# An mLSTM cell with a feed-forward block: the cells of chunks 2 to 5 beside groups 1 and 2, and groups 3 to 5 in three float32r parts

## The chip, the cores and the metric

The kernel runs on one core of one Trainium2 chip. The metric is the device time of one execution in microseconds. Before the change the median of three runs is 528.26 us (527.74 to 528.6).

A core has a matrix engine (TensorE, PE in the profile; the loading of its stationary operand is PEld), three engines for elementwise work (VectorE, DVE; ScalarE, ACT; GpSimd, POOL) and SyncE (SP), whose queue starts nearly all DMA transfers of this kernel. Each engine works through its own instructions in order and waits for the others by semaphores. SBUF is the on-chip memory, PSUM the memory into which TensorE writes, DRAM the memory outside.

## What is computed

The first half is a recurrent cell with a matrix state, 4 batches x 8 heads, 768 tokens, head dimension 40:

```
for t in range(S):
    m_new = maximum(f_gate[t] + m, i_gate[t])
    f_stab = exp(f_gate[t] + m - m_new);  i_stab = exp(i_gate[t] - m_new);  m = m_new
    C = f_stab * C + i_stab * outer(v[t], k[t])
    n = f_stab * n + i_stab * k[t]
    y[t] = sigmoid(o_gate[t]) * (C @ q[t]) / maximum(abs(n . q[t]), 1)
```

Its output, (B, H, S, D), becomes x of 3072 tokens x 320, and a feed-forward block follows: `h = x @ w_in` (320 x 2048), `g = max(0.01 h, h)`, `out = g @ w_out` (2048 x 320). Inputs are float32, the two weight matrices float64, which the kernel reads as 64-bit words and narrows to float32 itself.

## The kernel before

Tokens are cut into 6 chunks of 128. A *visit* s is one chunk c of one batch b (s = 4 c + b, 24 visits). The state of a batch passes from visit s to visit s + 4, so chunks follow each other. A *group* g of the feed-forward block is the 4 x 128 tokens of chunk g. In the main loop (L945) group c - 1 is computed beside the cells of chunk c, and the last group alone.

A group is a list of 32 units (`ff_units`). The first 16 are the entry: for each of 8 j, two units that together multiply x by two blocks of 128 columns of w_in (L743). x lies in `xT` in two halves of 64 rows, so the two blocks (r = 0 and 1) run as two matmuls of 64 rows and 512 columns side by side; ACT applies the leaky ReLU and writes `acts` (L751). The last 16 units are the exit: 16 matmuls of 320 columns for each 128 tokens (L778), a copy by ACT (L786) and a store (L787).

A visit of chunks 2 to 5 has two places where it uses TensorE:

- `u_parts` (scores L598, state update L603) needs the transposed keys and queries `kqT` (VectorE, L489), the decay weights `w` and `ku`, and gives `sd`; VectorE multiplies by `w` (L608) and adds to the state (L580).
- `u_mix` (L679) needs that, and gives `pT`. VectorE transposes it to `hb` (L686), forms the denominators (L617 to L619), multiplies by the output gate (L690), POOL by the denominators (L693), VectorE transposes to `x` (L697), and SP stores it in DRAM as `x_dr` (L700). `gather_x` reads it back into `xT` (L714).

After a u_mix of visit s comes `ahead(s + 2)`: kqT and `qn` of visit s + 2 (L489, L495), its `ku` and decayed state on POOL (L462, L576), and SP's loads of k, q and `ea` for visit s + 4. Then `load_late` and `feed` start o of visit s + 2 and k, v and `w` of visit s + 4. v goes in four transfers straight into the state tile S (L343). `prep_mask` adds the causal mask to w on POOL (L434), `prep_exp` takes the exponentials on ACT (L442).

`pairs` says after which unit of the group the cell units are done: two u_parts after unit 2, two u_mix after 6, two u_parts after 14, two u_mix after 19.

PE, DVE, ACT and POOL run in the order in which the code writes the instructions; SP's order is put together by the framework from when each transfer can start. `cells`, `wk`, `consts` and `gates` are pools of SBUF memory; all live for the whole kernel.

Of the kernel before, what the change touches and what calls it, by code (L numbers as in the profile page):

```python
# [9 lines left out]
F32 = mybir.dt.float32  # L10
U32 = mybir.dt.uint32
# [3 lines left out]
PSUM = bass.MemoryType.PSUM  # L15


@with_exitstack
def kernel(
# [51 lines left out]
    assert KR == DP and KC == 5 and KC * DP == Dm and GT * 4 <= 2048  # L71

    consts = ctx.enter_context(tc.tile_pool(name="consts", bufs=1))
    gp = ctx.enter_context(tc.tile_pool(name="gates", bufs=1))
    wk = ctx.enter_context(tc.tile_pool(name="wk", bufs=2))
    psf = ctx.enter_context(tc.tile_pool(name="psf", bufs=4, space=PSUM))
    psc = ctx.enter_context(tc.tile_pool(name="psc", bufs=4, space=PSUM))
# [47 lines left out]
    acts = consts.tile([P, NF, GT], F32, name="acts")  # L125
# [36 lines left out]
    QN = NF // 4  # L162
    QC = 4 * P
    WC = KC * 2 * P
    w_in = consts.tile([P, QN, WC], F32, name="w_in")
    w_out = consts.tile([P, NF, Dm], F32, name="w_out")
# [5 lines left out]
    def w_row(r, slot, j):  # L172
        n, e = divmod(j, 2)
        at = (2 * slot + e) * P
        return w_in[DP * r : DP * (r + 1), n, at : at + P]
# [6 lines left out]
    HW = 2 * Dm  # L182
    wide = moe_w_in.dtype == U64
    raws = {}
    if wide:
        raw_t = consts.tile([P, 5 * HW], U64, name="raw")

    def load_weights(n):

        m = n - QN  # L190
        if n < QN:
            dst = w_in[:, n, :]
        else:
            dst = w_out[:, 2 * m : 2 * m + 2, :].rearrange("p a d -> p (a d)")
        to = dst
        if wide:
            if n < 2:
                at = NF * GT - 2 * WC * (n + 1)
                raw = acts_l[:, at : at + 2 * WC].bitcast(U64)
            elif n < QN:  # L200
                raw = raw_t[:, WC * (n - 2) : WC * (n - 1)]
            elif m < 2:
                raw = w_out[:].rearrange("p f d -> p (f d)")[:, (2 + m) * WC : (3 + m) * WC].bitcast(U64)
            else:
                at = (4, 0, 1, 2, 3, 4)[m - 2] * HW
                raw = raw_t[:, at : at + HW]
            raws[n] = (raw, dst)
            to = raw
# [11 lines left out]
    def narrow_weights(n):  # L220
# [3 lines left out]
        if not wide:  # L224
            return
# [102 lines left out]
    def load(s):  # L328
# [12 lines left out]
        for u in range(2):  # L341
            for i in range(2):
                nc.sync.dma_start(  # L343
# [687 lines left out]
```

## Time and profile before

| | us |
|---|---|
| median of three runs | 528.26 |
| span of the profiled execution, first to last instruction | 526.4 |
| start to the first unit of group 1 | 139.64 |
| chunks 2, 3, 4, each with a group | 78.8 |
| chunk 5 with group 4 | 78.0 |
| group 5 alone, to the last instruction of TensorE | 69.3 |
| TensorE busy | 513.2 |
| VectorE, ACT, POOL busy in chunk 4 (78.76) | 32.7, 20.3, 17.4 |

The profile is one execution. "Busy" is the time in which an engine executes; an idle engine costs nothing unless the engine that sets the end waits for it. A matmul's weight load is a record of its own (PEld) and overlaps the matmuls before it. In a timeline a row is start, duration, engine, line and operation, and in brackets how long the engine stood idle before it and what ended that.

### The profile page before, as it was taken

To read this page: it belongs to the slowest core of one execution; us is meant where nothing else is said; L and a number is where in the kernel's file an instruction comes from. 1 tells how busy PE (TensorE), PEld (TensorE's weight loads), DVE (VectorE), ACT (ScalarE), POOL (GpSimd) and SP (SyncE) were. 2 spreads that over 40 slices of the span, in tenths; PEclk is the share of its full clock that TensorE was granted. 3 is DMA by queue.
4 is the path that set the end of the run, shared out by engine and by line. 5 is a ranking of instruction groups with operands and counts; after the bars stand their busy time and mean duration, and the time that the engine had idled before them with its cause. 6 is when DMAs were issued, how large, how long until landed. Compare 5 with 4: busy or idle time off the path is not lost.

```text
span 526.4 us, 11333 instructions
## 1 busy us (share of the span) xinstructions
PE 513.2 (97%) x4501; PEld 336.3 (64%) x4501; DVE 240.3 (46%) x431; ACT 168.1 (32%) x458; POOL 113.0 (21%) x145
## 2 busy tenths in 40 slices
PE   8889989999999999999999999999999999999997
PEld 7877878777555577555577555577554577544675
DVE  4679998999328446028445028344028230000000
ACT  4565865534534212034212124212125100122100
POOL 4244354152205121015021015021013010000000
PEclk9668999999999999999999999999999999999999
DMA  9977687888755626685626676626542112000000
GB/s 116 156 204 153 138 212 171 196 145 175 146 137 105 137 72 150 129 174 107 138 75 143 134 150 129 138 76 155 125 102 52 50 52 87 14 0 1 12 12 25
DMA packets 165284, 59.13 MB, mean 112 GB/s; under 512 B 128816, under 2 KB 156016, under 8 KB 165232
## 3 DMA queue, kind: packets, MB, share of 16 engines
q1 hardware_dynamic: 164848, 58.28, 51.0%
q8 instruction: 35, 0.57, 0.5%
q10 hardware_dynamic: 384, 0.13, 0.1%
q14 instruction: 17, 0.14, 0.1%
HBM read 51.68 MB, written 6.70 MB: 111 GB/s over the span
## 4 chain that ended last, share of the span: by engine, by line
PE 83%; SPq 6%; DVE 4%; DMA 2%; ACT 2%; issue 1%; POOL 1%; ACTq 0%; POOLq 0%
PE po L778 38%; PE ph L743 36%; PE pT L679 3%; SPq L213 3%; PE sd L598 3%; SPq L338 2%; SPq L352 1%; PE sd L603 1%; DMA rb<-in_q_dram 1%; DVE raw L245 1%; DVE qn L608 1%; DMA S<-in_v_dram 0%; DMA raw<-in_moe_w_in_dram 0%; PE tk L518 0%; PE hN L649 0%
## 5 line engine op out<-in xcount | busy, mean ns | idle before, releaser
L743 PE MATMUL ph<-xT,w_in 64*128 64x512 f32 (+1 forms) x1120 | 215.2, 536 | 0.6 <-ACT acts L751 0.6
L778 PE MATMUL po<-w_out,acts 128*128 128x320 f32 x768 | 211.1, 434 | 0.0
L778 PEld LDWEIGHTS po<-w_out,acts 128*128 128x128 f32 x768 | 144.5, 190 | 62.6 <-issue 4.1
L743 PEld LDWEIGHTS ph<-xT,w_in 64*128 64x128 f32 x1120 | 107.8, 189 | 94.4 <-issue 87.7
L751 ACT ACTIVATE acts<-ph 128x512 f32<-128x512 f32 (+1 forms) x112 | 53.9, 534 | 151.8 <-PE ph L743 151.7
L608 DVE TENSOR_TENSOR qn<-w,sd 64x512 f32<-64x512 f32 x40 | 27.4, 684 | 97.7 <-PE sd L603 57.1
L576 POOL TENSOR_TENSOR S<-S,f 40x336 f32<-40x336 f32 x36 | 30.9, 858 | 101.9 <-PE pT L679 65.8
L442 ACT ACTIVATE w<-w,gT 128x64 f32<-128x64 f32 (+1 forms) x192 | 51.1, 348 | 3.1 <-POOL w L434 2.1
L434 POOL TENSOR_TENSOR w<-w,i 128x512 f32<-128x512 f32 x20 | 28.1, 1411 | 104.7 <-ACT bu L294 53.0
L786 ACT COPY y<-po 128x320 f32<-128x320 f32 x12 | 5.1, 423 | 83.3 <-PE po L778 83.3
L786 ACT COPY hn<-po 128x320 f32<-128x320 f32 x12 | 5.1, 426 | 76.0 <-PE po L778 76.0
L686 DVE STREAM_TRANSPOSE hb<-pT 128x512 f32<-128x512 f32 x16 | 11.4, 714 | 39.2 <-PE pT L679 39.0
L495 DVE TENSOR_TENSOR qn<-kqT,ea 64x512 f32<-64x512 f32 x32 | 27.3, 854 | 0.9
L693 POOL TENSOR_TENSOR xb<-xb,den 128x320 f32<-128x320 f32 x16 | 11.7, 728 | 66.5 <-DVE xb L690 66.5
L598 PEld LDWEIGHTS sd<-kqT 40*64 40x64 f32 x640 | 19.9, 135 | 6.1 <-issue 6.1
L697 DVE STREAM_TRANSPOSE x<-xb 128x512 f32<-128x512 f32 x16 | 18.1, 1130 | 7.7 <-POOL xb L693 7.7
L598 PE MATMUL sd<-kqT 40*64 40x64 f32 x640 | 21.5, 220 | 0.0
L603 PE MATMUL sd<-S,vu 64*40 64x42 f32 x576 | 20.1, 214 | 0.7 <-POOL vu L462 0.7
L489 DVE STREAM_TRANSPOSE kqT<-rb 128x512 f32<-128x512 f32 x32 | 20.5, 677 | 0.0
L603 PEld LDWEIGHTS sd<-S,vu 64*40 64x40 f32 x576 | 18.6, 111 | 0.8 <-POOL vu L462 0.8
L580 DVE TENSOR_TENSOR S<-S,sd 40x336 f32<-40x336 f32 x36 | 18.1, 503 | 1.0
L679 PEld LDWEIGHTS pT<-qn,S 128*64 128x64 f32 x512 | 15.6, 138 | 3.6 <-issue 3.5
(126 smaller groups left out, 364.9 us busy)
## 6 DMA issues: line engine op xcount, KB each, us to landing
w<-a_dr SPq DMA_DIRECT2D x40, 128.0 KB
rb<-in_k_dram SPq DMA_DIRECT2D x64, 80.0 KB
rb<-in_q_dram SPq DMA_DIRECT2D x64, 80.0 KB
rb<-in_o_gate_dram SPq DMA_DIRECT2D x64, 80.0 KB
ea<-a_dr SPq DMA_DIRECT2D x32, 128.0 KB
kn<-in_k_dram SPq DMA_DIRECT2D x24, 160.0 KB
raw<-in_moe_w_out_dram SPq DMA_DIRECT2D x6, 640.0 KB
S<-in_v_dram SPq DMA_DIRECT2D x80, 40.0 KB
```

The source lines that it names most:

```text
L434: nc.gpsimd.tensor_tensor(w, w, cm2.unsqueeze(1).to_broadcast([P, H, SL]), op=ALU.add)
L442: yield nc.scalar.activation(w[:, h, :], w[:, h, :], AF.Exp, bias=gT[c][:, 0, bh : bh + 1], scale=1.0)
L489: nc.vector.transpose(d["kqT"][:, i].rearrange("p (h t n) -> p h n t", n=TS, t=QW), raw_blocks(s, i, QW).rearrange("p (h n) d -> p h n d", ...
L495: nc.vector.tensor_tensor(mixed(s)[rows, 1 - r], d["kqT"][rows, 1].rearrange("p (h t) -> p h t", t=SL), d["ea"][rows], op=ALU.mult,)
L576: nc.gpsimd.tensor_tensor(new, old, g, op=ALU.mult)
L598: nc.tensor.matmul(bank[1 - u][toks, h, :], lhsT=kqT[rows, 0, ts(h, SL)], rhs=kqT[rows, 1, ts(h, SL)], start=True, stop=True,)
L603: nc.tensor.matmul(dC[u][:, h].rearrange("p k d -> p (k d)"), lhsT=d["ku"][toks, h], rhs=S_v[s % NL][toks, u, h, :, :V1], start=True, stop ...
L608: nc.vector.tensor_tensor(mixed(s)[toks, u], w[toks], bank[1 - u][toks], op=ALU.mult)
L679: nc.tensor.matmul(pT[DP * r : DP * (r + 1), j * P + u * SL : j * P + (u + 1) * SL], lhsT=S[:, u, h, :], rhs=m[:, u, h, :], start=True, st ...
L743: nc.tensor.matmul(ph[r][:, cols], lhsT=w_row(r, slot, j), rhs=xT[DP * r : DP * (r + 1), slot, cols], start=(slot == 0), stop=(slot == KC ...
L751: nc.scalar.activation(acts[:, f, cols], ph[r][:, cols], AF.Prelu, alpha=0.01)
L778: nc.tensor.matmul(po[n][:], lhsT=acts[:, f, ts(n, P)], rhs=w_out[:, f, :], start=(f == 0), stop=(f == NF - 1),)
```

## The change

- **Order of the work.** Each of the chunks 2 to 5 now runs beside 16 units instead of 32: chunks 2 and 3 beside group 1, 4 and 5 beside group 2. `pairs` becomes (1, 1, 5, 5, 9, 9, 13, 13, 13), `masks` {0: (2, 3), 8: (4, 5)}. x of group 2 is gathered in units 0 to 3 of chunk 3. After the last u_mix two units of group 2 are left.
- **Memory.** What only the cells use lies in pools on the right side that are closed after chunk 5; the parts of groups 3 to 5 (pool `late`) take that memory tile by tile. xT, acts, weights and y are in a pool `fp` that stays, where new tiles take the place of old ones by tag (xa in xT, wi0 in raw_a, wo0 in w_in3, wo12 in acts, g0 in raw_b, g3 in w_out).
- **v.** One transfer for each visit, into the unused half of its w tile; POOL copies it into S in two instructions ahead of the mask.
- **Groups 3 to 5** go in half-groups of 256 tokens (hg 6 to 11), 8 steps u each. A step is one entry of two blocks in one PSUM tile and, two steps later (LAG), its exit. Each operand a is split: h keeps the upper 12 bits of the mantissa (a mask), low = a - h. A product is put together from three float32r matmuls: h by h, low by 4096 low, and one of the combinations h (1 + 1/4096) - a with 4096 low - h; the last two sum up in one bank, the first in another, and ACT and DVE join them as (1 + 1/4096) x first + second. Weights are split once (`split_w`: w_in's first quarter in chunk 3, the others and w_out from the end of group 2 into group 3), x for each half-group (`split_x`), the activations for each step of groups 4 and 5 (`grow`). In group 3 the exit is still f32 from the unsplit activations (`whole`).

```diff
-            for u in range(2): for i in range(2): nc.sync.dma_start(S_v[n][ts(u, SL), u, :, i, :DB], v[...])
+        w = wk.tile([P, H, P], F32, name="w", bufs=NL)[:].rearrange("p h t -> p (h t)")
+        nc.sync.dma_start(w[:, H * SL : H * SL + Dm]..., v[b, :, rows, :].rearrange("h p d -> p h d"))
...
 def prep_mask(s):
+        for u in range(2):
+            nc.gpsimd.tensor_copy(S_v[s % NL][ts(u, SL), u, :, :, :DB], st[s]["v"][ts(u, SL)])
         nc.gpsimd.tensor_tensor(w, w, cm2.unsqueeze(1).to_broadcast([P, H, SL]), op=ALU.add)
...
+        def split_w(w, parts):
+            nc.vector.tensor_scalar(h.bitcast(U32), w.bitcast(U32), scalar1=HIGH, scalar2=None, op0=ALU.bitwise_and)
+            yield
+            nc.scalar.copy(parts[0], h)
+            nc.gpsimd.tensor_tensor(low, w, h, op=ALU.subtract)
+            yield
+            nc.scalar.activation(parts[1], low, AF.Copy, scale=SPLIT)
+            yield
+            nc.vector.scalar_tensor_tensor(parts[2], in0=low, scalar=SPLIT, in1=h, op0=ALU.mult, op1=ALU.subtract)
+            yield
...
+        ffs = ff_units(1)
+        for c in range(2, NB):
+            cells, done, fed = cell_units(c), 0, 0
+            for i in range(UC):
+                if at == len(ffs):
+                    ffs, at = ff_units(2), 0
+                exponents()
...
+                ffs[at]()
+                at += 1
...
+                visits(c, i)
+                if c == 3 and i < B:
+                    gather_x(2 * B + i)
+                fetches()
+                if c == NB - 1 and i == pairs[-1]:
+                    break
+        cell.close()
...
+        def split_x(hg):
+            to = xs[hg % 2]
+            for at, n in ((0, 3), (3, 2)):
+                h = late_p.tile([P, 3, GH], F32, name="xh")
+                x, h = xf[:, at : at + n, :], h[:, :n, :]
+                nc.vector.tensor_scalar(h.bitcast(U32), x.bitcast(U32), scalar1=HIGH, scalar2=None, op0=ALU.bitwise_and)
+                nc.scalar.copy(to[0][:, at : at + n, :], h)
+                nc.gpsimd.tensor_tensor(to[1][:, at : at + n, :], x, h, op=ALU.subtract)
+                nc.vector.scalar_tensor_tensor(to[2][:, at : at + n, :], in0=h, scalar=JOIN, in1=x, op0=ALU.mult, op1=ALU.subtract)
+                yield
...
+        load_x(HG0)
+        first = split_x(HG0)
+        now = splits()
+        while at < len(ffs):
+            ffs[at]()
+            at += 1
+            run(first, 1)
+            run(now, 3)
...
+        def enter(u):
+            ph = psh.tile([P, 2, 2, GH], F32, name="p3")
+            for v in range(3):
+                for slot in range(KC):
+                    for r in range(2):
+                        nc.tensor.matmul(ph[:, r, v // 2, :], lhsT=w[rows, v, c0 : c0 + P], rhs=x[v][rows, slot, :], ...)
+            nc.scalar.activation(a, ph[:, :, 0, :], AF.Copy, scale=JOIN)
+            nc.vector.tensor_tensor(a, a, ph[:, :, 1, :], op=ALU.add)
+            nc.scalar.activation(a, a, AF.Prelu, alpha=0.01)
...
+        def grow(u):
+            nc.vector.tensor_scalar(h.bitcast(U32), a.bitcast(U32), scalar1=HIGH, scalar2=None, op0=ALU.bitwise_and)
+            nc.scalar.copy(g[:, 0], h)
+            nc.vector.tensor_tensor(g[:, 1], a, h, op=ALU.subtract)
+            nc.vector.scalar_tensor_tensor(g[:, 2], in0=h, scalar=JOIN, in1=a, op0=ALU.mult, op1=ALU.subtract)
...
+        def leave(u):
+            for n in range(HB):
+                for r in range(2):
+                    for v in range(1 if whole else 3):
+                        nc.tensor.matmul(p[:, v // 2, :Dm], lhsT=lhsT, rhs=rhs, ...)
+                if j == NJ - 1:
+                    if whole:
+                        nc.scalar.copy(y[:], p[:, 0, :Dm])
+                    else:
+                        nc.scalar.activation(y[:], p[:, 0, :Dm], AF.Copy, scale=JOIN)
+                        nc.vector.tensor_tensor(y[:], y[:], p[:, 1, :Dm], op=ALU.add)
+                    nc.sync.dma_start(out[row : row + P, :], y[:])
+
+        for u in range(HG0 * NJ, HG2 * NJ + LAG):
+            hg, j = divmod(u, NJ)
+            if HG1 * NJ < u <= HG2 * NJ:
+                grow(u - 1)
+            if hg < HG1:
+                run(now, 3)
+            if u < HG2 * NJ:
+                enter(u)
+            if hg + 1 < HG2:
+                if j == 2:
+                    first = split_x(hg + 1)
+                if j in (2, 4):
+                    run(first, 1)
+                if j == 4 and hg + 2 < HG2:
+                    run(first, 1)
+                    load_x(hg + 2)
+            if u - LAG >= HG0 * NJ:
+                leave(u - LAG)
```

In the changed kernel's orders the weight splits and the x split of the switch stand as the code writes them: on VectorE the mask and second product of x's first three slots, the mask of w_in's second quarter, then x's last two slots; on ACT the copy of the first three slots, both ACT parts of that quarter, an out copy, then the copy of the last two slots.

## The prediction

> **What bounds the kernel now.** I read the page's busy line first, then the busy time by stretches of the span, then the groups by form, the timeline of one visit, and SP's timeline.
>
> ```profile
> PE 513.2 (97%) x4501; PEld 336.3 (64%) x4501; DVE 240.3 (46%) x431; ACT 168.1 (32%) x458; POOL 113.0 (21%) x145
> ```
>
> ```profile
> 60.00:139.64 79.64, 77.31 (x1059) 60.70 (x1054) 71.50 (x106) 44.91 (x122) 30.47 (x27) 1.00 0.82 174
> ...
> 297.23:375.99 78.76, 78.76 (x680) 47.77 (x680) 32.74 (x58) 20.29 (x60) 17.36 (x20) 1.00 0.59 131
> ...
> 454.03:526.40 72.37, 69.19 (x289) 39.57 (x288) 0.00 (x0) 10.81 (x21) 0.00 (x0) 0.99 0.03 12
> ```
>
> The first is the page's busy line, the second the stretches; there the columns are PE, PEld, DVE, ACT, POOL, clock, DMA share, GB/s. From 139.6 us on TensorE never waits: a group with a chunk of cells beside it lasts 78.8 us, the last group alone 69.2 us. So a chunk's cells hold TensorE 9.6 us (chunk 5, without a state update: 78.0 - 69.2 = 8.8), a feed-forward unit takes 69.2/32 = 2.16 us, and only cheaper products can shorten this part. Everything else is slack there, and the change spends that slack.
>
> ```profile
> L778 PE MATMUL po<-w_out,acts 128*128 128x320 f32 x768 | 211.1, 434 | 0.0
> L743 PE MATMUL ph<-xT,w_in 64*128 64x512 f32 x800 | 176.3, 593 | 0.0
> ...
> L679 PE MATMUL pT<-qn,S 128*64 128x64 f32 x512 | 16.7, 224 | 0.0
> ```
>
> The program issues 384 matmuls at L778, the trace has 768 records: an f32 matmul is two records. One of 320 columns costs 211.1/384 = 0.55 us. The short ones at L679 cost 16.7/256 = 65 ns each.
>
> **Part 1: chunks 2 to 5 beside groups 1 and 2.** The first 139.6 us keep their order. There v needs 12 fewer SP issues and POOL gets two copies a visit; I take 0, bounds -3 and +3. After that 62 units (134.1 us) and the cells (3 x 9.6 + 8.8 = 37.6) are 171.7 us of TensorE. A chunk now lasts about 44 us instead of 78.8, so all its other work must fit 44.
>
> ```profile
> 316.22 0.72 DVE L686 STREAM_TRANSPOSE hb<-pT 128x512 f32<-128x512 f32 x1 [6.93 <-PE pT L679]
> ...
> 317.61 0.49 DVE L690 SCALAR_TENSOR_TENSOR xb<-rb,hb 128x320 f32<-128x320 f32 x1
> ...
> 319.00 1.16 DVE L697 STREAM_TRANSPOSE x<-xb 128x512 f32<-128x512 f32 x1 [0.37 <-POOL xb L693]
> ...
> 319.99 1.29 DVE L489 STREAM_TRANSPOSE kqT<-rb 128x512 f32<-128x512 f32 x2
> ...
> 321.31 1.39 DVE L495 TENSOR_TENSOR qn<-kqT,ea 64x512 f32<-64x512 f32 x2
> ...
> 326.48 1.27 DVE L489 STREAM_TRANSPOSE kqT<-rb 128x512 f32<-128x512 f32 x2
> 327.09 2.95 POOL L434 TENSOR_TENSOR w<-w,i 128x512 f32<-128x512 f32 x2
> ...
> 327.78 2.81 DVE L495 TENSOR_TENSOR qn<-kqT,ea 64x512 f32<-64x512 f32 x2
> ```
>
> This is VectorE after a u_mix. From 316.22 to the second visit's kqT (326.48 + 1.27) are 11.5 us. In the old kernel eight units followed; now four do (pairs 5 to 9), 8.65 us plus the second u_mix's 1 us, then u_parts of the first new visit, 1.05 us: 10.7 us. TensorE stands in line behind u_parts and waits 1 us. The last two rows show the same two products doubled (1.39 to 2.81 us) beside POOL's mask, and the masks and v copies (two of about 0.5 us, between L149's copy, 0.23, and L462, 0.72; POOL rises from 17.4 to some 21 of 44 us, hidden but for this effect) now fall into that stretch: 2.5 us at the upper end. I take 1.6 for each of seven handovers, 11 us (bounds 0 and 18).
>
> ```profile
> 302.56 0.39 SPq L340 DMA_DIRECT2D kn<-in_k_dram  x1
> 303.04 2.68 SPq L343 DMA_DIRECT2D S<-in_v_dram  x4
> ...
> 320.22 1.47 SPq L700 DMA_DIRECT2D x_dr<-x  x4
> 321.79 1.79 SPq L382 DMA_DIRECT2D rb<-in_k_dram  x4
> ...
> 340.85 5.14 SPq L714 DMA_DIRECT2D xT<-x_dr  x8
> ```
>
> SP issues for 69.9 of the 78.8 us of this chunk. The change takes 3 of 4 v issues away: the one that remains has kn's form, 0.39 + 0.1 between. A visit keeps x_dr, k, q, ea, o, w, kn, v: 1.6 + 1.9 + 2.0 + 1.2 + 2.1 + 1.4 + 0.5 + 0.5 = 11.2 us, a chunk 45 us and about 47 with the gates and out. That is what TensorE and its waits take (44 + 3), so SP just keeps up. In chunk 3 the 16 gathers for group 2 (2 x 5.14 us) come on top, ahead of the x_dr of visit 12. The o of visit 14, which had about 3 us to spare, comes some 7 us late, VectorE's xb waits for it, and the next kqT and u_parts with it: 7 us (bounds 0 and 12). The Trainium skill ("DMA: Bandwidth & Descriptors", Issuing engines are not separate DMA queues) says that the sequencer's time to start a DMA is usually small beside the DMA; by it these 7 us would be 0 and the total below 533. The rows, 0.37 to 0.67 us for each issue at a queue that is 89% full, speak against that rule here. DMA work itself was 0.59 of 78.8 = 46 us a chunk; without the gathers, half of the stores and half of v's packets I count it at 36 of 47.
>
> **Part 2: the switch.** After the last u_mix (call its end T) only two units, 4.3 us, are left for TensorE, and the next thing in its order is group 3's first entry, which needs x in parts. VectorE first finishes two visits (2 x 3.75 from T - 1, to T + 7). The scratch tile of the first split lies in the memory of visit 23's x, so the split waits for that x to be stored: four issues 1.5 us, landing about 2 (an estimate from the last out store, 2.65 us from issue to the end): T + 11. Then, in the engines' orders, mask 0.6, the second product 0.95, mask of w_in's quarter 0.82 on VectorE, POOL's 1280-element difference (four times L462's 0.72 = 2.9), ACT's scaling of it (1.37, as L231 at 1280) and the out copy 0.43, and only behind them ACT's copy of x's last two slots (0.63): T + 18.7. TensorE is idle 14 us (bounds 6 and 20). The clock fell to 0.5 to 0.6 in the page's slices around 20 to 40 us, where work was thin; 4 us at half clock after the gap are 2 us.
>
> **Part 3: products in three parts.** No row shows a float32r matmul. An f32 product of 24-bit mantissas is four products of 12-bit halves, so the lower end is a quarter of the f32 matmul: 0.55/4 = 0.138 us for 320 columns. The upper end is one whole record, 0.275. I take the quarter: masked operands carry 12 bits, and one part product is all that each needs. The skill ("FP8 and Floating Point Precision", TensorE Precision Notes) gives true FP32 four passes and describes a reduced reading of 4-byte FP32; it states no rate for it. An entry is 30 matmuls of 256 columns in pairs: 15 x 0.107 = 1.6 us by the quarter of 2.13, but 30 x 65 ns = 1.95 by L679's rate of issue; I take 1.9. An exit is 12 x 0.138 = 1.65 us (f32: 4 x 0.533 = 2.13). In group 3 exits stay f32: 16 entries and 14 exits 60.3 us, against 69.2.
>
> Seven weight splits run there, each on one scratch: mask 0.82, POOL 2.9, ACT 1.37, 5.1 us in series, three of four steps to a step of TensorE (3.8 us of 4.0). ACT's evacuation of the entry stands behind ACT's scaling, which waits for POOL: the first four steps lose 3.3 us, the next five 0.7 each: 7 us (bounds 2 and 14).
>
> In groups 4 and 5 each of 32 steps costs TensorE 1.9 + 1.65 = 3.55 us. VectorE does per step an add from PSUM (0.68, L608), a mask (0.42, L243's slope 0.52 ns an element), a difference and a second product (0.69 each, L495 undisturbed), 0.1 between, and waits for ACT's leaky ReLU between add and mask (0.6 + 0.1): 3.28, with the x splits 3.45. Nearly tied; 32 x 3.55 = 113.6 us (bounds 105 and 131), 24.8 less than the 138.4 of f32. Loads of x (8 issues, 5.1 us a half-group of 28) are hidden.
>
> **The end.** Add to last part 2.5, last exit 1.4, copy and add 1.0, store 2.65: 7.6 us, against 526.4 - 523.3 = 3.1.
>
> **The sum.** 139.6 + 171.7 + 11 + 7 + 4.3 + 14 + 2 + 60.3 + 7 + 113.6 + 7.6 = 538.1 us of span, against 526.4. The median shown, 528.26, lies 1.9 above the span, so I predict 540.
>
> **Rivals.**
> - *The cells' stage stays bound by TensorE, so the change gains.* Place: handovers in chunks 2 to 5. If VectorE's way from pT to the second kqT stays under 10.7 us (POOL not in the way) and o is never late, the 18 us of waits go: 520 + 2 = 522. For it: 11.5 against 10.7 is close, and SP's loads are ordered a half chunk ahead. Against: the doubled rows. It decides from 6 us of waits on, below which the total is under 528. With the kinder ends of entry (1.6) and the gap (10) it reaches 510. Chance 0.3.
> - *VectorE sets groups 4 and 5.* If the round trip add, ReLU, mask and the x splits fill up to 4.1 us a step, as the row L241 (0.82 at 640) and longer hops would have it, 32 x 0.55 = 18 more: 558. For it: 3.45 against 3.55. Against: POOL is idle there, and L495 undisturbed is 0.69. Chance 0.13.
> - *Three parts aren't cheaper.* If a float32r matmul costs a whole record, an entry is 3.2 and an exit 3.3 us: 32 x 6.5 = 208 and group 3 81, total 655. For it: no row shows the contrary. Chance 0.05.
>
> **How the numbers follow.** The forecast has 0.52: its own range is 526 to 553, a twentieth of it at or below the old time. About 0.2% (1 us) is what a measurement can tell from no change. Faster: 0.3 of the first rival and 0.01 of the forecast; the same 0.04, from the forecast's lower edge; slower 0.65. The range takes in the lower bounds of waits and gap and the second rival: 511 to 563.
>
> **What would show it.** Right: idle TensorE of 10 us or more after the last unit of group 2, ended by ACT's copy of xs; u_parts waiting for VectorE's kqT once a half chunk; 256-column float32r matmuls about 65 ns apart; steps of 3.5 us in groups 4 and 5. Wrong: a chunk of 45 us without waits; matmuls of 320 columns at 0.27 us; a step above 4 us.

## The result, and the profile after

| | us | ratio to before |
|---|---|---|
| before, median of four runs | 528.0 (527.33 to 528.6) | |
| after, median of four runs | 607.9 (605.93 to 612.29) | 1.1526, 95% interval 1.1481 to 1.1571 |
| predicted | 540 (511 to 563) | 1.02 |

The change is slower, as forecast, but by 80 us and not by 12. The busy line of the page after, and the busy time by stretches (columns as in the prediction: PE, PEld, DVE, ACT, POOL, clock, DMA share, GB/s):

```profile
PE 530.3 (87%) x5589; PEld 405.7 (67%) x5589; DVE 377.2 (62%) x623; ACT 246.0 (41%) x566; POOL 183.3 (30%) x205
```

```profile
60.00:148.16 88.16, 80.94 (x1072) 63.42 (x1071) 75.17 (x112) 44.29 (x121) 39.73 (x42) 0.95 0.68 162
148.16:379.46 231.30, 193.62 (x2066) 121.75 (x2066) 122.88 (x232) 60.48 (x186) 70.60 (x93) 0.88 0.54 125
379.46:442.36 62.90, 42.11 (x329) 32.83 (x328) 34.70 (x33) 30.23 (x37) 29.82 (x12) 0.78 0.10 28
...
481.50:597.60 116.10, 116.10 (x1249) 106.47 (x1249) 87.40 (x137) 58.81 (x102) 12.90 (x6) 1.00 0.08 24
```

TensorE, which never waited after 139.6 us before, is now idle for 38 us in the cells' stage (second row, 231.30 - 193.62) and for 21 us at the switch (third row). All of the 38 us are waits for the transposed keys and queries (what waited, for what: us in total, times, longest):

```profile
PE sd L611 <- DVE kqT L502: 37.7, 10, 7.2
```

In both rows its clock is below 1 too, and its busy time is longer for the same work: up to the end of the last u_mix 189.1 us for the 171.7 that the prediction summed. In groups 4 and 5 (last row) it never waits.

The sum of the prediction against the profiled execution (span 607.1):

| term | predicted | measured | more |
|---|---|---|---|
| start, to group 1's first unit | 139.6 | 148.2 | 8.6 |
| cells' stage, to the end of the last u_mix at 374.97: work 171.7, waits 11 + 7 | 189.7 | 226.8 | 37.1 |
| two last units | 4.3 | 4.5 | 0.2 |
| gap 14, clock 2, split stalls 7 | 23 | 28.7 | 5.7 |
| to the first three-part exit: 19 entries, 16 f32 exits | 70.2 | 75.2 | 5.0 |
| 29 steps of groups 4 and 5 | 103.0 | 114.2 | 11.2 |
| the rest | 8.3 | 9.5 | 1.2 |
| sum | 538.1 | 607.1 | 69.0 |

The fourth measured term is what the stretch from 379.46 to 483.38 leaves beside 19 entries of 1.98 and 16 exits of 2.35 us, 75.2 together: 20.8 us in which TensorE is idle, and 7.9 by which its busy time (83.1) is longer than those 75.2. More than half of the miss is in the stage of the cells, so most experiments went there.

### The profile page after: what moved, and what is told of

It is laid out like the page before. It is cut to its first block, busy times and chain, and to the rows that moved or that the text cites. A ratio compares the mean times of both kernels' runs of the same rounds, so it can differ in the third digit from the quotient of the medians.

```text
span 607.1 us, 13916 instructions
## 1 busy us (share of the span) xinstructions
PE 530.3 (87%) x5589; PEld 405.7 (67%) x5589; DVE 377.2 (62%) x623; ACT 246.0 (41%) x566; POOL 183.3 (30%) x205
## 4 chain that ended last, share of the span: by engine, by line
PE 38%; DVE 20%; SPq 15%; DMA 10%; POOL 7%; issue 6%; ACT 2%; ACTq 0%; DVEq 0%; POOLq 0%
PE so L1181 14%; PE p L1141 13%; PE ph L759 6%; SPq L395 5%; DMA w<-a_dr 4%; POOL raw_b L967 3%; DVE kqT L502 3%; SPq L228 3%; DMA w<-in_v_dram 2%; DVE qn L508 2%; PE po L794 2%; PE sd L611 2%; SPq L351 2%; SPq L408 2%; DVE qn L621 1%
## 5 line engine op out<-in xcount | busy, mean ns | idle before, releaser
L759 PE MATMUL ph<-xT,w_in 64*128 64x256 f32 (+1 forms) x640 | 118.1, 522 | 4.7 <-ACT xT L745 3.5
L1141 PE MATMUL p<-xs,wi 64*128 64x256 f32 x1440 | 103.5, 295 | 20.8 <-ACT xs L1103 13.0
L1141 PEld LDWEIGHTS p<-xs,wi 64*128 64x128 f32 x1440 | 93.4, 195 | 34.7 <-ACT xs L1103 13.8
L794 PE MATMUL po<-w_out,acts 128*128 128x320 f32 x384 | 113.0, 451 | 0.0
L759 PEld LDWEIGHTS ph<-xT,w_in 64*128 64x128 f32 x640 | 65.4, 202 | 48.3 <-issue 37.4
L794 PEld LDWEIGHTS po<-w_out,acts 128*128 128x128 f32 x384 | 74.4, 198 | 32.2 <-issue 5.2
L1181 PE MATMUL so<-wo,g 128*128 128x320 f32 x384 | 64.4, 317 | 0.0
L611 PE MATMUL sd<-kqT 40*64 40x64 f32 x640 | 28.6, 253 | 37.7 <-DVE kqT L502 37.7
L1104 POOL TENSOR_TENSOR xs<-xa,xh 128x768 fp32r<-128x768 f32 (+1 forms) x12 | 25.8, 2154 | 117.1 <-DVE xh L1102 95.4
L1181 PEld LDWEIGHTS so<-wo,g 128*128 128x128 f32 x384 | 56.3, 188 | 4.2 <-DVE g L1164 0.2
L767 ACT ACTIVATE acts<-ph 128x256 f32<-128x256 f32 (+1 forms) x64 | 27.9, 487 | 76.7 <-PE ph L759 76.6
L589 POOL TENSOR_TENSOR S<-S,f 40x336 f32<-40x336 f32 x36 | 31.5, 876 | 57.5 <-PE hN L662 29.4
L446 POOL COPY S<-w 64x320 f32<-64x320 f32 x40 | 21.2, 531 | 81.8 <-DMA w<-in_v_dram 80.6
L1146 DVE TENSOR_TENSOR ar<-ar,p 128x512 f32<-128x512 f32 x24 | 16.4, 684 | 29.5 <-ACT ar L1145 29.5
L699 DVE STREAM_TRANSPOSE hb<-pT 128x512 f32<-128x512 f32 x16 | 11.4, 714 | 32.7 <-PE pT L692 32.5
```

Source lines behind the costliest of these rows:

```text
L589: nc.gpsimd.tensor_tensor(new, old, g, op=ALU.mult)
L611: nc.tensor.matmul(bank[1 - u][toks, h, :], lhsT=kqT[rows, 0, ts(h, SL)], rhs=kqT[rows, 1, ts(h, SL)], start=True, stop=True,)
L759: nc.tensor.matmul(ph[r][:, cols], lhsT=w_row(r, slot, j), rhs=xT[DP * r : DP * (r + 1), slot, cols], start=(slot == 0), stop=(slot == KC ...
L767: nc.scalar.activation(acts[:, f, cols], ph[r][:, cols], AF.Prelu, alpha=0.01)
L794: nc.tensor.matmul(po[n][:], lhsT=acts[:, f, ts(n, P)], rhs=w_out[:, f, :], start=(f == 0), stop=(f == NF - 1),)
L1141: nc.tensor.matmul(ph[:, r, v // 2, :], lhsT=w[rows, v, c0 : c0 + P], rhs=x[v][rows, slot, :], start=(slot == 0 and v != 1), stop=(slot == ...
```

## The experiments

Each is an edit of the changed kernel unless a base is named; "stage" is the time from group 1's first unit to the end of the last u_mix in the profiled execution.

**What holds the cells' stage.** A half chunk of the changed kernel as SP issues (start, duration, line, transfer) and as POOL works (in brackets how long it stood idle, and what ended that):

```profile
270.32 1.63 SPq L713 DMA_DIRECT2D x_dr<-x  x4
...
279.10 0.58 SPq L357 DMA_DIRECT2D w<-in_v_dram  x1
279.74 1.59 SPq L408 DMA_DIRECT2D w<-a_dr  x2
...
284.10 0.88 SPq L357 DMA_DIRECT2D w<-in_v_dram  x1
285.03 2.34 SPq L408 DMA_DIRECT2D w<-a_dr  x2
...
293.97 1.45 SPq L713 DMA_DIRECT2D x_dr<-x  x4
```

```profile
283.78 0.95 POOL L446 COPY S<-w 64x320 f32<-64x320 f32 x2 [13.06 <-DMA w<-in_v_dram]
284.88 1.27 POOL L447 TENSOR_TENSOR w<-w,i 128x512 f32<-128x512 f32 x1
288.53 0.95 POOL L446 COPY S<-w 64x320 f32<-64x320 f32 x2 [2.38 <-DMA w<-in_v_dram]
289.88 1.27 POOL L447 TENSOR_TENSOR w<-w,i 128x512 f32<-128x512 f32 x1 [0.39 <-DMA w<-a_dr]
291.22 0.77 POOL L589 TENSOR_TENSOR S<-S,f 40x336 f32<-40x336 f32 x1
292.07 0.73 POOL L706 TENSOR_TENSOR xb<-xb,den 128x320 f32<-128x320 f32 x1
```

The reader sees a closed loop. POOL stands 13 us in front of a v copy whose transfer SP issued at 279.10, behind the x stores of the u_mix before; behind that copy in POOL's order stand the mask, the state product (L589) and xb (L706) of the *next* u_mix; from xb VectorE makes the x that SP stores at 293.97; and only behind that store come the next v loads. In VectorE's order the next kqT stands behind that x too, and so TensorE waits with them. A turn takes 293.97 - 263.71 = 30.3 us (263.71 is the first x store of the half chunk), against 21.5 of TensorE work. In the old kernel these masks came 6 and 13 units after the u_mix that lets the loads start, now both come 3 units after it. Three edits cut the loop at different places.

First, the old path of v back, without the copies:

```diff
+            for u in range(2): for i in range(2): nc.sync.dma_start(S_v[n][...], v[b, ...])
-        nc.sync.dma_start(w[:, H * SL : H * SL + Dm]..., v[b, :, rows, :]...)
-            nc.gpsimd.tensor_copy(S_v[s % NL][...], st[s]["v"][...])
```

> The changed kernel with the old path of v: four transfers of each visit straight into S, no copies on POOL. Theory (POOL's order waits for w as well, which SP issues right behind v; the list only grows by 2.2 us a visit): 610 to 630 us, POOL's wait is then for w. Rival (the copies on POOL are the cause): half chunks of 25 us, total below 590.

624.8 us, stage 245.2. The waits of this run and, below, of the changed kernel (what waited, for what: us in total, times, longest):

```profile
POOL w L447 <- DMA w<-a_dr: 122.6, 11, 19.0
```

```profile
POOL S L446 <- DMA w<-in_v_dram: 80.6, 10, 16.6
```

So the copies alone are not the cause. Without them POOL's mask waits at the same place, longer, for w, which SP issues behind v; and SP's list has grown by three issues a visit. The new path of v gains 17 us against the old one in this order.

Second, the masks later in POOL's order, third, the loads earlier in SP's:

```diff
-        masks = {0: (2, 3), 8: (4, 5)}
+        masks = {6: (2, 3), 14: (4, 5)}
```

> The masks and v copies of POOL are issued six units later (after the u_mix of the half chunk, not before it). Theory A, order on POOL: the v copy of the next pair waits for a v load that SP issues behind the x stores, and the state product and xb product of u_mix stand behind it on POOL, so that one half chunk takes a whole turn of SP's list (30.3 us now). Then the half chunk falls to about 24 to 26 us, the stage of the cells from 226.7 to 190 to 205 us, the total to 572 to 590 us, and POOL's 80 us of waiting for v fall below 30. Theory B, SP's list alone sets the turn (22.7 us of issues and the wait for x): the stage shrinks by less than 10 us, total 598 or more. Theory C, POOL's masks slow VectorE's products more there: 608 or more.

```diff
-                if fn in (u_mix, u_plain): load_late(s + NR, 2); if s + NL < NS: feed(s + NL)
+                if fn in (u_mix, u_plain): load_late(s + NR, 2)
+                if (fn is u_plain or fn is u_parts and s >= 2 * B) and s + NL < NS: feed(s + NL)
```

> POOL's order stays; SP issues kn, v and w of the visit four later after u_parts, that is ahead of the x stores of this pair, not behind them. Theory A (v arrives too late for POOL's order): the wait for v goes as well, half chunks of 24 to 27 us, total 575 to 592 us. Theory B (length of SP's list): the list is as long, 600 us or more. A rival inside A: SP now waits at the head of its queue for the w buffer of u_parts, which delays the o load; then it is 595 or more with ACT waiting for o.

Masks later: 597.6 us (596.65 to 598.61), stage 219.8. That misses theory A's range and lies at the edge of theory B's (598 or more, the stage less than 10 us shorter; it is 7.0). POOL's waits for v are gone (0.6 us), but what follows the mask now waits for POOL (from 148 to 380 us):

```profile
ACT w L455 <- POOL w L447: 60.1, 14, 7.5
...
PE sd L616 <- POOL S L446: 25.2, 24, 5.9
```

So this run alone leaves A and B open. Loads earlier: 585.7 us (585.22 to 586.11), stage 206.3, as theory A has it, 22 us less with a list as long. POOL's waits for v are down to 1.6 us; what is left on TensorE is the wait that the prediction had named, near its size (18 us there):

```profile
ACT rb L491 <- DMA rb<-in_o_gate_dram: 35.9, 7, 16.5
...
PE sd L611 <- DVE kqT L502: 22.7, 9, 5.3
```

**The start.** ACT's third out copy (L799) waited 5.0 us for an out store, and xT copies stood behind it.

```diff
-                y = fp.tile([P, Dm], F32, name="y", bufs=2)[:]
+                if n < 2 or g == 2: y = fp.tile([P, Dm], F32, name="y", bufs=2)[:]
+                else: y = wk.tile([P, H, D1], F32, name="hn")[:].rearrange("p h d -> p (h d)")[:, :Dm]
```

> The out copies of batches 2 and 3 of groups 0 and 1 go to the cells' hn buffers again, as in the kernel before, not to the two y buffers. Theory: ACT's out copy waits for an earlier out store and the xT copies stand behind it; group 1 starts at 139.5 to 141 us, not at 148.2, and the total falls by 7 to 9 us, to 599 to 601. Rival, the new v path delays chunk 1's cells: the start stays at 147 or later and the total at 605 or more.

599.6 us (598.34 to 600.86), 8.3 less, but group 1 starts at 143.47, not at 140: the rest of the gain is later. And the start is not a fixed quantity: with the masks later, where the first stage is the same code as in the changed kernel and ACT waits as long for the store (5.1 us), group 1 began at 141.92. Over all profiled executions it begins at 141.92 to 148.16 us with the two buffers (seven runs) and at 137.93 to 144.37 without (twelve). Together with the early loads the gain is not seen:

> Early v loads and hn buffers together, which the runs on the gathers, the split order, the shift, ACT's o loads and VectorE's differences were compared with by a sum of 577.3 us only. If the two gains add, 575 to 579 us. If the half chunk after the start takes back what the start gained (in the run with VectorE's differences x of visit 8 was stored only 2.2 us earlier than without the hn buffers), 581 to 585.

585.1 us median of five (four of 583.99 to 585.44, one of 578.87, which is the profiled one, with a start at 139.77 and a stage of 204.3). So in the totals the two buffers cost 8 us in the changed kernel and nothing that is seen behind the early loads; where the difference goes is not shown. This run is the *base* of the following ones; those that ran before it were expected against the sum, 577.3, and have to be read against 585.1.

**What holds the stage then: SP's list, or VectorE's way.** Two edits moved issues from SP to ACT:

```diff
-        gather(s, st["xT", c], ts(b, P))
+        gather(s, st["xT", c], ts(b, P), nc.scalar)
```

> As the run with the early v loads (585.7 us), with the hn buffers for the out copies (8.3 us less, alone), and with the 16 gathers of group 2's x in chunk 3 issued by ACT in place of SP. Theory (the gathers stand on SP ahead of x's stores and of the loads of o, and cost the half chunk of 37.8 us about 13): 577.3 - 10 to 14, that is 563 to 568 us, that half chunk at 24 to 27 us. Rival (the transfers themselves crowd the DMA engines, whoever issues them, or ACT is held up by issuing): 573 to 580 us.

583.3 us (582.27 to 584.25), stage 208.2: no gain. The half chunk with the gathers still takes 37.1 us between x stores, now because four issues of k take SP 10.25 us, and the o loads behind them come late by as much. What SP waited for there is not shown by the profile.

```diff
-                nc.sync.dma_start(rb_t[s % NR][rows, i, ...], part)
+                (nc.scalar if i == 2 else nc.sync).dma_start(rb_t[s % NR][rows, i, ...], part)
```

> Early v loads and hn buffers (577.3 us by sum), and the loads of o in blocks (8 issues of the 46 to 48 in a half chunk) are issued by ACT, not by SP. Theory (with v out of the way, SP's list of some 22 us against TensorE's 21.5 a half chunk is what is left, and o, last in it, comes late): total 560 to 570, half chunks at 22 to 24 us, ACT's wait for o below 15 us. Rival (ACT, which waits for VectorE's xb before it may issue, holds up the leaky ReLUs of the units; or o is late for the transfers, not for the issue): 575 or more.

595.6 us (593.09 to 598.09): the rival. ACT is held at its own issues, with o named as the releaser: 29.5 us ahead of leaky ReLUs, 51 ahead of out copies. Then the cover of VectorE's way was lengthened by a unit:

```diff
-        pairs = (1, 1, 5, 5, 9, 9, 13, 13, 13)
+        pairs = (1, 1, 4, 4, 9, 9, 12, 12, 12)
```

> Early v loads and hn buffers (577.3 us by sum of the two runs), and each u_mix is issued one unit earlier, so that five units follow it in place of four ahead of the next u_parts, and three in place of four stand between u_parts and u_mix. Theory (VectorE's way from pT to the second kqT is longer than the four units that cover it; 22.7 us of waits for kqT were left in the run with early v loads): each of the waits shrinks by up to 2.2 us, total 562 to 570. Rival (the way from u_parts to u_mix is as tight, or SP's list of issues sets the turn): the wait moves to pT or to o, total 575 to 582.

588.6 us (588.24 to 588.97), no better than the base, with ACT's wait for o up to 63.1 us. That fits a list in which o comes last, and asks for the two causes one at a time:

```diff
-        elif s < NS:
+        elif s < NS and (i < 2 or s < 2 * B + NR):
             load_blocks(s, i)
```

> As the base (early v loads, hn buffers) without the loads of o from visit 10 on; the gate of o then uses stale values (the output is not the reference's). SP's list of a half chunk is 8 issues, some 4 us, shorter, and 3 MB of transfers fall away. Theory (SP's list, with o last, is what holds the stage after v is mended): half chunks of 22 to 23 us from visit 12 on, 15 us or more below the base. Rival (VectorE's way from pT to kqT against four units of cover): less than 6 us below the base, with the waits for kqT still near 20 us.

> As the run without the loads of o, with u_mix one unit earlier, so that five units cover VectorE's way. In the run that had the shift but all loads, ACT waited 63 us for o, and the total rose. If both limits are there, o's lateness hid the gain of the shift: now the waits for kqT fall below 12 us, and the total is 5 to 12 us below the run without o loads. If SP's list alone holds the stage: within 3 us of it.

559.6 us (559.53 to 559.70), 25.5 below the base: SP's list with o in it. TensorE's waits for kqT fell from 22.7 us to 6.8. In the base VectorE's xb had waited for ACT's gate of o, which waits for the load; this wait is gone:

```profile
DVE xb L703 <- ACT rb L491: 15.3, 3, 9.9
```

With the shift 549.8 us (549.77 to 549.78), another 9.8 less. The stretch 250 to 300 us of the changed kernel and of this run:

```profile
250.00:300.00 50.00, 36.62 (x438) 20.84 (x437) 26.56 (x54) 16.14 (x51) 19.87 (x27) 0.90 0.65 142
```

```profile
250.00:300.00 50.00, 50.00 (x600) 32.23 (x598) 35.48 (x68) 19.15 (x64) 21.27 (x29) 1.00 0.69 155
```

TensorE never waits, at full clock, while the DMA engines are no less busy. The stage is 170.7 us. The shift leaves three units behind the last u_mix and not two, so one unit of 2.16 us lies outside this stage: of the 171.7 us of pure TensorE work that the prediction had summed 169.5 are left in it, and TensorE is busy for 169.7. So both of its named waits existed, but the late o is worth some 25 us and not 7, and VectorE's way some 9 (182.4 - 2.2 - 170.7). Leaving o out also takes its transfers away; the run with o issued by POOL (below) keeps them, and its stage is 180.9 us against 204.0 for the shift with o on SP (the edits at the switch, which it has too, touch one weight split of this stage). So most of it is the issuing and not the transfers.

The profiled executions also show that a wait costs more than its length. What the stage had beside TensorE's work, in us (171.7, with the shift 169.5):

| | stage | idle | busy beyond the work | clock |
|---|---|---|---|---|
| changed kernel | 226.8 | 37.7 | 17.4 | 0.88 |
| loads earlier | 206.3 | 22.9 | 11.6 | 0.93 |
| base | 204.3 | 23.0 | 9.6 | 0.94 |
| without o | 182.4 | 7.3 | 3.3 | 0.99 |
| without o, with the shift | 170.7 | 1.0 | 0.2 | 1.00 |

It is no fixed rate: with the masks later, 25.2 us of idle in many short waits stand beside 22.9 us of longer busy time.

**The switch.** VectorE there, in the changed kernel (start, duration):

```profile
384.30 0.56 DVE L1102 TENSOR_SCALAR xh<-xa 128x768 uint32<-128x768 uint32 x1 [2.79 <-DMA x_dr<-x]
...
385.77 2.44 DVE L964 TENSOR_SCALAR raw_b<-w_in 128x1280 uint32<-128x1280 uint32 x1
...
388.58 3.26 DVE L1105 SCALAR_TENSOR_TENSOR xs<-xh,xa 128x512 fp32r<-128x512 f32 x1
391.76 2.55 DVE L971 SCALAR_TENSOR_TENSOR wi<-raw_b 128x1280 fp32r<-128x1280 f32 x1
```

TensorE and POOL in the same stretch:

```profile
385.85 1.01 PE L1141 MATMUL p<-xs,wi 64*128 64x256 f32 x6 [6.39 <-ACT xs L1103]
393.48 6.11 PE L1141 MATMUL p<-xs,wi 64*128 64x256 f32 x54 [6.61 <-ACT xs L1103]
```

```profile
384.99 2.53 POOL L1104 TENSOR_TENSOR xs<-xa,xh 128x768 fp32r<-128x768 f32 x1 [4.61 <-DVE xh L1102]
388.29 3.00 POOL L967 TENSOR_TENSOR raw_b<-w_in,raw_b 128x1280 f32<-128x1280 f32 x1 [0.76 <-DVE raw_b L964]
```

TensorE is idle 6.39 and 6.61 us here, 13.0 (predicted 14). But three VectorE rows (2.44, 3.26, 2.55) are longer than foreseen, while POOL's differences run. Two edits on the base: x split whole before the weights, and the differences given to VectorE.

```diff
-            run(first, 1)
-            run(now, 3)
+            run(first, 1)
...
-            nc.gpsimd.tensor_tensor(low, w, h, op=ALU.subtract)
+            nc.vector.tensor_tensor(low, w, h, op=ALU.subtract)
-                nc.gpsimd.tensor_tensor(to[1][...], x, h, op=ALU.subtract)
+                nc.vector.tensor_tensor(to[1][...], x, h, op=ALU.subtract)
```

> Early v loads and hn buffers as before (577.3 us by sum), and at the switch both halves of x are split ahead of the weights' splits, not between them. Theory (the second half of x waits behind the weight's mask on VectorE and its difference on POOL): the gap of 13.5 us shrinks to 7 to 9, total 571 to 574. Rival (the weights' splits are the bound, they only start later, and TensorE waits for them at the third step): total 576 or more, with the idle time moved to the next steps.

> Early v loads and hn buffers (577.3 us by sum), and the differences of the splits, of the weights and of x, are done by VectorE, POOL has none. Theory (each weight split waits for POOL's 2.9 us, and VectorE's mask and product are up to four times slower beside POOL: 2.44 for 0.83, 3.25 for 0.69): the gap of 13.5 us shrinks to 9 to 11, the stalls of the splits, 10 us idle and 6 us at a lower clock, to less than half; total 564 to 571. Rival (VectorE's longer list delays its adds from PSUM as much): 575 or more.

> Early v loads, hn buffers, x split in whole ahead of the weights, all differences on VectorE. If the two edits at the switch each took away part of its 13.5 us of gap and its stalls, total 566 to 572 us; if they removed the same wait, 572 to 577. No theory lets it pass the 528.3 us of the kernel before.

Split order: 576.4 us (573.67 to 579.03); the gap shrinks to 8.7 us from 13.5 in the base, and the steps of group 3 behind it wait 11.4 us, little less than there (12.2). The two runs of it reach up to the lowest of the base (578.87), so alone its gain is not settled. Differences on VectorE: 572.9 (572.50 to 573.27), 12 below the base. Both: 564.8 (562.91 to 565.90), 20 below it. VectorE with both edits (its lines stand three further down):

```profile
358.59 0.68 DVE L1108 SCALAR_TENSOR_TENSOR xs<-xh,xa 128x512 fp32r<-128x512 f32 x1
359.19 0.82 DVE L967 TENSOR_SCALAR raw_b<-w_in 128x1280 uint32<-128x1280 uint32 x1
360.05 1.49 DVE L970 TENSOR_TENSOR raw_b<-w_in,raw_b 128x1280 f32<-128x1280 f32 x1
```

The product takes 0.68 in place of 3.26 us, the mask 0.82 in place of 2.44, and the difference itself 1.49, where POOL took 2.92. The Trainium skill ("SBUF — State Buffer", SBUF: two separate sides) states that VectorE, in some operations, and GpSimd take a shared port pair exclusively for a whole instruction; the rows agree: 3.26 is 0.68 and most of POOL's 3.00.

**The products.** Groups 3 to 5 in f32, in the same half groups, no splits:

```diff
-        HG0, HG1, HG2 = 6, 8, 2 * NB
+        HG0, HG1, HG2 = 6, 2 * NB, 2 * NB
...
-                            ph[:, r, v // 2, :], lhsT=w[rows, v, c0 : c0 + P], rhs=x[v][rows, slot, :],
+                        ph[:, r, 0, :], lhsT=w[rows, c0 : c0 + P], rhs=x[rows, slot, :],
```

> The stage of the cells is untouched, but groups 3 to 5 are done in plain f32 in the same half groups, without any splits. Theory (three parts gain 0.34 us in each of 32 steps, 11 us, and lose about as much to gap and split stalls): idle of 5 to 8 us after the last unit, 48 steps of 4.3 us = 206, end 4, total 595 to 605, no slower than the 607.9 with parts. Rival (the parts pay, their stalls are small): total 612 to 622.

621.4 us (618.64 to 624.10): the theory falls, the parts pay by 13.5 us in spite of gap and splits. Where it went wrong is seen in a steady step: 2.36 us for an f32 entry and 2.35 for an exit, 4.71 together, not 4.3. The old order had 25 entry matmuls of 512 columns in 10.89 us, which makes 2.18 for ten of 256. So half groups and alternation together cost f32 about 0.4 us a step by themselves.

The size of a float32r matmul, by columns:

```diff
-                            ph[:, r, v // 2, :], lhsT=..., rhs=x[v][rows, slot, :],
+                            ph[:, r, v // 2, : GH // 2], lhsT=..., rhs=x[v][rows, slot, : GH // 2],
...
+                        if hg >= HG1 + 2: rhs = rhs[:, : Dm // 2]
```

> Measures a float32r matmul by size. Of the changed kernel, entries of groups 3 to 5 multiply 128 of 256 columns and exits of groups 4 and 5 but the first two half groups' worth of steps... that is of the last two half groups 160 of 320 columns; the results left out are filled with copies, so the output is not the reference's. Theory (an entry's matmul stands at an issue floor of 66 ns, whatever its columns; an exit's matmul is 0.417 ns a column plus a fixed 26 ns): entry bursts of 30 stay at 1.95 to 2.0 us, exit bursts of 12 fall from 1.95 to 1.1 us (93 ns each). Rival 1, time by columns alone: entries 1.0 to 1.1 us, exits 0.98. Rival 2, the weight load of 128 columns sets both: entries as now, exits stay above 1.7 us.

647.4 us (one run), slower though it multiplies less. Entries of 128 columns went from burst to burst in 1.82 us at full clock, 61 ns each, against 1.98: half the columns take 8% off, as a floor would have it. But when the short exits came in as well, the clock fell to 0.50 in a wait of 2.44 us and stayed there, with TensorE busy all the time from then on:

```profile
553.25 2.85 PE L1185 MATMUL so<-wo,g 128*128 128x160 f32 x12 [2.44 <-DVE y L1199]
```

```profile
560.00:620.00 60.00, 60.00 (x411) 57.50 (x412) 29.87 (x58) 22.10 (x46) 1.72 (x1) 0.50 0.02 6
```

After a wait of 2.45 us before 519.18, with exits of 320 columns behind it, the clock was 0.55 up to 522.5 us and 1.00 from there. So the exits were sized again with full entries beside them:

```diff
+                        if hg == HG1 + 2: rhs = rhs[:, : Dm // 2]
+                        if hg == HG1 + 3: rhs = three["out", f // HV][:, v].rearrange("p a d -> p (a d)")[:, at : at + 480]
```

> Sizes an exit's float32r matmul at full clock. Of the changed kernel, the exits of the last but one half group multiply 160 columns and those of the last 480, where 320 are needed (the output of these is not the reference's); entries stay. At 320 columns a burst of 12 takes 1.95 us, 163 ns each. Theory (0.417 ns a column, the quarter that the prediction took, plus a fixed 26 to 30 ns for each matmul): 12 of 160 columns 1.13 to 1.17 us, 12 of 480 2.72 to 2.76. Rival (a rate of 0.51 ns a column, no fixed part): 0.98 and 2.94. Second rival (a floor of the weights' load or issue): 160 columns at 1.4 us or more, 480 at 2.4 to 2.75.

The bursts of 12, of 320, 160 and 480 columns. A burst is read to the start of the next one (537.43, 540.92 and 575.74), which is 0.07 us before its listed end:

```profile
535.48 2.02 PE L1186 MATMUL so<-wo,g 128*128 128x320 f32 x12
537.43 2.06 PE L1141 MATMUL p<-xs,wi 64*128 64x256 f32 x30
539.42 1.57 PE L1186 MATMUL so<-wo,g 128*128 128x160 f32 x12
...
572.93 2.88 PE L1186 MATMUL so<-wo,g 128*128 128x480 f32 x12
```

That is 162 ns at 320 columns, 125 at 160 and 234 at 480. At the 0.417 ns a column of the theory the two longer ones leave 29 and 34 ns fixed, so 480 columns take a little longer than it said (2.81 us against 2.72 to 2.76); the line through both has 0.448 ns a column and 19 ns fixed. Two sizes cannot tell these apart. At 160 columns that line would give 91 ns; the 125 measured is the second rival's floor. The skill ("TensorE: Matmul & The Clock Gate", LDWEIGHTS (loading the stationary operand)) sets a weight load by the stationary's columns alone, by its formula an estimate of 107 ns for 128 columns; the two floors are nearly equal, as such a rule would have it, but higher: 125 ns for 128 rows, and 2 x 61 for a pair of 64 rows side by side.

**What can be had.** All gains in one kernel, with the o loads in blocks issued by POOL behind the product that frees their buffer; and the same without the o loads from visit 10 on:

```diff
-                nc.sync.dma_start(rb_t[s % NR][rows, i, ...], part)
+                (nc.gpsimd if i == 2 else nc.sync).dma_start(rb_t[s % NR][rows, i, ...], part)
```

> All edits that gained, in one kernel with the reference's output: early v loads, hn buffers, u_mix one unit earlier, x split in whole first, differences on VectorE, and the loads of o in blocks issued by POOL, right behind the xb product that frees their buffer, so that SP's list is 8 issues shorter a half chunk and no engine waits to issue. Theory (SP's list held the stage): 530 to 545 us. Rival (an issue by POOL costs it more than SP's 0.46 us, and POOL's masks and products come late): 555 or more. In either case not below 526.

> The same, but the loads of o from visit 10 on are left out (stale gates, the output is not the reference's) and none is on POOL: what the change could give at best with TensorE never waiting in the cells' stage. From the run without o loads and with the shift (549.8 us) less the 20 us that the edits at the switch gained: 527 to 533 us, about the kernel before. If the edits at the switch gain less there, 533 to 540.

541.6 us (539.59 to 545.70), ratio to before 1.0288 (1.0240 to 1.0335), stage 180.9; and 533.1 (531.09 to 535.99), ratio 1.0105 (1.0064 to 1.0147), stage 174.2. An issue costs POOL 0.55 us; SP's issues of k and q have a median of 0.45 from 180 to 260 us of the same run. No version tried is below the kernel before: in the bound run the way from the last u_mix to the end is 217.4 us; three units, three groups in the old form and the old end would be 6.5 + 3 x 69.2 + 3.1 = 217.2. What the parts save in the steps is spent at the switch and by the dearer steps, and TensorE's work before it is the same in either order.

## Why the prediction was right in sign and wrong in size

- **v and the masks (part 1).** The failed step. It said of v: 12 fewer issues, POOL gets two copies a visit, "I take 0", and later only weighed the copies as load beside VectorE. It did not ask what stands *behind* the new waiting instruction on POOL, nor when the w and v loads are issued relative to a mask that now comes 3 units after a u_mix. The early loads show 22 us for it, with POOL's 80.6 us of waiting for v down to 1.6. The copies alone are not it (old path: 624.8, POOL waits for w instead).
- **Late o, "7 us (bounds 0 and 12)".** The mechanism held, but not only in chunk 3: a list of 22 us a half chunk against 21.5 of TensorE leaves no slack anywhere. Without the o loads the time falls by 25.5 us, twice the upper bound, in the way named: xb waits for the gate of o, and kqT behind it. The rule of the skill weighed there ("DMA: Bandwidth & Descriptors", Issuing engines are not separate DMA queues) would have said 0; in these runs issuing decides (stage 204.0 us with o issued by SP, 180.9 by POOL).
- **Handovers, "1.6 us for each of seven".** Right in kind and near in size (11 us): 9.8 by the shift, once o was out of the way, 9.4 of it in the stage.
- **The clock in the stage, taken as full.** The sum has work and waits only. With the waits of the changed kernel TensorE's busy time there is 17.4 us longer than the work, at a clock of 0.88. Part of what the early loads and the missing o gain is this time.
- **TensorE's work, 171.7 us.** Right: in the run where nothing waited TensorE is busy for 169.7, of 169.5 without the unit that the shift moves behind the stage. So the first rival's stage exists, but only with the early loads, the shift and 8 issues less a half chunk.
- **Start, taken as 0 ± 3.** That two out buffers now serve where four did was overlooked. How much of the 8.6 us it is stays open: 8.3 us in one comparison of totals, nothing seen behind the early loads. The start also varies by itself: 138.25 us in the run with ACT's gathers and 143.51 in the one with the shift, whose code is the same up to there.
- **Gap, 14 us.** Right (13.0), with its chain: x of visit 23 awaited 2.79 us, ACT's copy of x ends it. But the doubled rows which the prediction had found beside POOL's mask were not applied to the splits, which run beside POOL's 2.9 us; 12 us come back when the differences leave POOL.
- **Splits and clock, 7 and 2 us.** The steps of group 3 were idle 7.8 us (20.8 less the gap), as taken; the clock cost 7.9 and not 2, because it stayed low past the gap (0.78 from 379.46 to 442.36).
- **Entries 1.9 us.** 1.98, right: 66 ns each. The row of L679 gave the number, not the reason: a floor that is 125 ns for 128 rows is no common issue rate. That the number fits is in part luck.
- **Exits, 12 x 0.138.** 162 ns each at 320 columns, so the third rival's 0.275 us falls; a fixed part beside the columns was missing: 1.95 us, and 0.3 us in each of 32 steps is 9.6 us. The 2.13 us taken for an f32 exit of four stands in no row (the prediction's own 0.55 us makes 2.20); between entries it took 2.35.
- **VectorE in groups 4 and 5.** As forecast not the bound: 87.40 of 116.10 us, rows of 0.43 and 0.69. The second rival's time of a step (4.1) was nearly met (3.94), for another reason.

The named waits, at the handovers and for o, are there (both shown), but they do not carry the sign alone. By the first rival the total without them would be 522 us; the run where TensorE never waited in the stage took 549.8. From the last u_mix to the end the changed kernel takes 232.1 us where the sum has 208.8, and even the bound run, with the better switch, only comes level with the old form there (217.4 against 217.2). So the sign would have been the same without the waits, which the prediction did not foresee. The size was off mainly by a wait that the sum had put at nothing, on POOL. In the profiled executions the waits and what came with them add 53.9 us to the stage (226.8 - 170.7 - 2.2), where the sum had 18: 20.5 go with the early loads, 22.0 with o, 9.4 with the shift, and 2.0 between two runs that differ in the out buffers.

## What to carry to other kernels

When a stage is made shorter, list for each engine what stands behind every instruction that waits for a transfer, and when that transfer is issued in the new order: a wait at the head of an elementwise engine's queue can close a loop through the DMA queue that no busy share shows. Count issues in a queue as work: at about half a microsecond each, 47 of them are as long as the half chunk that they feed. Price a wait of TensorE at more than its length where its clock falls with it: 37.7 us of idle came with 17.4 us of slower work here. An operation's cost taken from long runs of it need not hold when short runs of two kinds alternate (4.71 us a step here, not 4.3).

## What was not expected of the hardware

- With matmuls of 128 columns (64 rows) and 160 columns (128 rows) in turn, after a wait of 2.44 us, TensorE was busy 60.00 of 60 us and its clock stayed at 0.50 (one run). With 256 and 160 columns it was 1.00, but no such wait came before. The clock gate page of the skill ("TensorE: Matmul & The Clock Gate", What's actually happening) ties the clock to how busy the engine was; here being busy, as the profile counts it, did not bring the clock back.
- A float32r matmul of 128 rows took 125 ns at 160 columns, where the line through 320 and 480 columns would give 91.
- VectorE's product of 512 elements took 3.26 us instead of 0.68 while POOL's difference of 1280 ran.
- The granted clock falls with short waits too: in 230 to 240 us of the changed kernel, after a wait of 7.19 us and with one of 4.53 in it, it was 0.50, and 1.00 again from 245 us.
